# Ten weight units' rounded high part, written by a transfer from GpSimd instead of a copy on ScalarE

## The chip, the cores and the metric

The kernel runs on one core of one Trainium2 chip. The metric is the device time of one execution in microseconds (us); three runs of the kernel before gave 872.08, 871.21 and 870.69, median 871.21. A core has a matrix engine, TensorE (PE; its weight loads are listed apart as PEld), VectorE (DVE), ScalarE (ACT), GpSimd (POOL) and SyncE (SP). Each engine runs its own queue in order and waits for the others by semaphores. SP issues transfers here; after the change GpSimd does too. Results of PE land in PSUM; everything else between the steps lies in SBUF, 128 partitions wide.

## The reference

Attention in which both softmaxes come ahead of the products, followed by a dense two-layer network with the Mish function:

```python
def _attn_ref(q, k, v):            # (8, 8, 576, 64) each
    q_s = q - np.max(q, axis=-1, keepdims=True)
    q_s = np.exp(q_s)
    q_s = q_s / (np.sum(q_s, axis=-1, keepdims=True) + 1e-09)
    k_s = k - np.max(k, axis=2, keepdims=True)
    k_s = np.exp(k_s)
    k_s = k_s / (np.sum(k_s, axis=2, keepdims=True) + 1e-09)
    kv = np.einsum('bhsd,bhse->bhde', k_s, v)
    return np.einsum('bhsd,bhde->bhse', q_s, kv)

def _moe_ref(x, w_in, w_out):      # x: (4608, 512), w_in: (512, 2048), w_out: (2048, 512)
    h = x @ w_in
    sp = np.where(h > 20.0, h, np.log1p(np.exp(np.minimum(h, 20.0))))
    g = h * np.tanh(sp)
    return g @ w_out
```

x is the attention's output, heads side by side. The two weight matrices come as 64-bit floats.

## The kernel before, in words

The 4608 tokens are taken in 9 groups of 512. For each group, x is made from attention items (two heads at a time), then for 16 blocks n of 128 hidden columns: a product with w_in (`h_part`, four parts of 128 rows each), Mish on ACT (`g_mish`, "Y"), a rounded high part gh and a remainder gl (`g_hi`, `g_lo`), and a product with w_out (`out_mm`, "O"), three blocks behind. PE takes factors of the type float32r; to keep their accuracy, each factor is split in a high part (the value rounded to float32r) and a low part (value minus high part), and each product is three matmuls: high with high, high with low, low with high. So PE's third matmul of each `h_part` needs the low part of w_in (tile wil), the first two the high part (wih); in `out_mm` the first needs the high part of a w_out block (tile wo) and the second its low part.

The weights are converted on the chip. They come in 32 units of 128x512 weights: an "in" unit holds 128 columns of w_in, and its result goes into the tiles wih and wil as 128x4x128 (four pieces of 128 numbers per partition); an "out" unit holds 128 rows of w_out, and its result is a tile wo with both parts, 512 numbers in a row per partition each. The steps of unit j, each a token with its number:

- R: a load of the raw 64-bit words by SP (tiles raw_in, raw_out; line 110).
- RA: the upper word's magnitude, scaled, on ACT, into a tile wc_in or wc_out (line 117). These tiles share four buffers, so RA waits until an earlier unit's last step has freed one.
- RL or RM: the lower word, scaled, on ACT (line 121) or DVE (line 125).
- RB, then RC: the bits of both put together, then the sign, on DVE (lines 129 and 133). After RC the unit's float32 value stands in wc.
- RH: the high part, a copy on ACT into float32r (line 146, `w_hi`), shown as CAST.
- RO or RD: the low part, value minus high part, on GpSimd or DVE (line 97, `w_lo`).

From unit 17 on the units alternate: 17 in, 18 out, 19 in, 20 out and so on to 27 in; 28 to 31 are out. While the first tokens are worked on, all this is mixed with the attention items and with the first group's products. The order is not planned by rules: the string FIRST lists every step as a token, in the order of issue, and each engine's queue is the tokens that fall on it, in that order (`tc.manual_schedule`). H40 is the `h_part` of block 10, part 0 (40 = 4 x 10 + 0), and it is the first to need unit 17; H60 is block 15, part 0, the first to need unit 27. O8 and O12 are the products of out units 20 and 28; H56 is block 14, part 0. From about 130 us on the products run alone with the last attention items.

Other steps that stand beside the change: KS is the subtraction of the k maximum on DVE (line 265), E the two exponentials ke and qe on ACT (line 280), which take a table load on ACT before them, and another before the Mish that follows; Q is the q sum on DVE (lines 300 to 304) with its multiplication on GpSimd (line 309); K is the product of ke with v on PE (pkv, line 290).

Of the kernel before, what the change touches and what calls it, by code (L numbers as in the profile page):

```python
# [9 lines left out]
F32R = mybir.dt.float32r  # L10
# [30 lines left out]

STAGED = (
# [5 lines left out]
def attn_mish_mlp(ctx: ExitStack, tc: tile.TileContext, q, k, v, wu, qs, kt, out):  # L48
# [3 lines left out]
    nc = tc.nc  # L52
# [43 lines left out]
    def sub(eng, out, a, b):  # L96
        eng.tensor_tensor(out, a, b, ALU.subtract)  # L97
# [37 lines left out]
    def w_dst(j):  # L135
        kind, f = units[j]
        a = conv[j][2].bitcast(F32)
        if kind == "out" and f not in wo:
            wo[f] = xp.tile([P, 2, DM], F32R, tag=f"wo{f}", name=f"wo{f}")
        if kind == "in":  # L140
            return a.rearrange("p (t c) -> p t c", t=HP), [w[:, :, f * P:(f + 1) * P] for w in wi]
        return a, [wo[f][:, 0], wo[f][:, 1]]

    def w_hi(j):
        a, d = w_dst(j)
        nc.scalar.copy(d[0], a)  # L146

    def w_lo(j, eng):
        a, d = w_dst(j)
        sub(eng, d[1], a, d[0].bitcast(F32))  # L150
        conv.pop(j)
# [293 lines left out]
    def x_lo(i, src):  # L445
        nc.vector.tensor_tensor(xs[i][:, 1], src, xs[i][:, 0].bitcast(F32), ALU.subtract)  # L446
# [11 lines left out]
    def h_part(n, t):  # L458
        c, f = divmod(n, NF)
        if t == 0:  # L460
            gs[n] = ps_h.tile([P, 512], F32, tag="h", name=f"ph{n}")
        fs = slice(f * P, (f + 1) * P)
        x = xs[c * HP + t]
        for i, (a, z) in enumerate(((0, 0), (0, 1), (1, 0))):
            nc.tensor.matmul(gs[n], wi[a][:, t, fs], x[:, z], start=t == 0 and i == 0,  # L465
                             stop=t == HP - 1 and i == 2)
# [26 lines left out]
    def g_hi(n, copy=nc.vector.tensor_copy):  # L493
        hi = pools["rp"].tile([P, SM], F32R, tag="rh", name=f"gh{n}")
        copy(hi, gs[n])  # L495
        gs[n] = gs[n], hi
# [33 lines left out]
    def group(n):  # L530
# [58 lines left out]
        L=k_load, LK=kt_load, LQ=q_load, V=v_load, R=w_load, MK=a_kmx, MQ=a_qmax, SQ=a_qsub, SD=lambda i: a_qsub(i, nc.vector), B=a_kmax, KS=a_ksub, EK=lambda i: a_exp(i, "k"), EQ=lambda i: a_exp(i, "q"), E=a_exp, K=a_kv,  # L589
        Q=a_qsum, QM=a_qmul, QD=lambda i: a_qmul(i, nc.vector), S=a_ksum, SA=lambda i: a_kvs(i, i < HP), SB=lambda i: a_kvs(i, True), T=a_qt, TC=a_qt2, X=a_x, Z=lambda i: x_hi(i, at[i]["px"]),  # L590
        ZL=lambda i: x_lo(i, at[i]["px"]), ZT=a_tail2, ST=a_tail3, RA=w_abs, RL=w_low, RM=w_low_v, RB=w_bits, RC=w_sign,
        RH=w_hi, RO=lambda j: w_lo(j, nc.gpsimd), RD=lambda j: w_lo(j, nc.vector),
        H=lambda x: h_part(x // HP, x % HP), Y=g_mish, G=g_hi, GA=lambda n: g_hi(n, nc.scalar.copy), GL=g_lo, O=out_mm)
    with tc.manual_schedule(engines={ET.Activation, ET.PE, ET.DVE, ET.Pool, ET.SP}):
        for token in first:
# [53 lines left out]
```

## Time and profile before

| | |
|---|---|
| times of three runs | 872.08, 871.21, 870.69 us |
| profiled execution | 871.54 us, of which 869.8 us from the first to the last instruction |
| granted TensorE clock | 0.996 |
| PE, DVE, ACT, POOL busy | 848.1, 475.3, 336.4, 92.3 us |
| casts of line 146 | 32, of some 0.62 us each |
| transfers issued by GpSimd | none |

The profile is of one execution. Its page gives busy time by engine, the groups of instructions and the transfers; the timelines of one engine give for each instruction its start and length in us, its engine and line, the tile it writes and the tiles it reads, and in brackets how long the engine had idled and who released it. Equal neighbours stand in one row (x2, x3). A busy PE row of x2 holds two matmuls, of some 0.23 us each.

### The profile page before, as it was taken

The page shows a single profiled execution, that of the slowest core. Times are in us where ns is not written, and L with a number is a line of the kernel's source. Part 1 is how long each engine was busy: PE and PEld are TensorE (multiplying, and loading weights), DVE is VectorE, ACT ScalarE, POOL GpSimd, SP SyncE. Part 2 cuts the span into 40 slices and gives each one's busy share as a digit, 9 for nine tenths or more (in the row PEclk, how much of TensorE's full clock was granted, in tenths as well). Part 3 has the DMA queues.
Part 4 walks back from the last instruction along what each step waited for, and adds up shares of the span by engine and source line. Part 5 has one row for each costly group of instructions (what it writes and reads, how often), then busy time and mean ns, then how long its engine had stood idle before and what let it go on. Part 6 is the DMA issues. An engine that isn't in the chain of part 4 may idle for free.

```text
span 869.8 us, 11465 instructions
## 1 busy us (share of the span) xinstructions
PE 848.1 (98%) x4368; PEld 685.5 (79%) x4368; DVE 475.3 (55%) x1196; ACT 336.4 (39%) x509; POOL 92.3 (11%) x91
## 2 busy tenths in 40 slices
PE   5999999999999999999999999999999999999998
PEld 3677777787888878787878787878888788888886
DVE  6899997656474746465565556564743222222221
ACT  4999873424243333424342424242432111111111
POOL 4024221111111001111010111111110000000000
PEclk9899999999999999999999999999999999999999
DMA  9975344222232223212231222222200020001001
GB/s 306 388 248 194 106 132 122 71 49 60 63 103 47 72 47 105 63 54 65 91 77 31 74 76 69 51 60 61 76 18 1 15 73 13 1 0 49 1 1 49
DMA packets 73975, 69.16 MB, mean 80 GB/s; under 512 B 52928, under 2 KB 52928, under 8 KB 73920
## 3 DMA queue, kind: packets, MB, share of 16 engines
q1 hardware_dynamic: 73600, 67.91, 26.4%
q8 instruction: 34, 0.56, 0.3%
q10 hardware_dynamic: 320, 0.52, 0.2%
q14 instruction: 21, 0.17, 0.1%
HBM read 57.93 MB, written 10.49 MB: 79 GB/s over the span
## 4 chain that ended last, share of the span: by engine, by line
PE 89%; ACT 6%; SPq 1%; DVE 1%; issue 1%; DMA 1%; ACTq 0%; DVEq 0%
PE po L515 43%; PE ph L465 43%; PE pt L392 2%; PE px L380 1%; ACT L490 1%; DMA kt<-in_kt_dram 1%; ACT raw_out L121 1%; ACT wc_out L117 1%; ACT raw_in L121 1%; ACT y L490 1%; PE px L365 1%; ACT L280 0%; ACT wo L146 0%; SPq L171 0%; ACT wih L146 0%
## 5 line engine op out<-in xcount | busy, mean ns | idle before, releaser
L465 PE MATMUL ph<-xs,wih 128*128 128x512 f32 x1152 | 358.7, 393 | 3.8 <-ACT y L490 3.8
L515 PE MATMUL po<-wo,gh 128*128 128x512 f32 x1152 | 355.6, 390 | 0.3 <-POOL wo L97 0.3
L465 PEld LDWEIGHTS ph<-xs,wih 128*128 128x128 f32 x1152 | 214.0, 188 | 50.4 <-ACT y L490 5.2
L515 PEld LDWEIGHTS po<-wo,gh 128*128 128x128 f32 x1152 | 216.2, 188 | 45.5 <-POOL wo L97 0.6
L465 PE MATMUL ph<-xs,wil 128*128 128x512 f32 x576 | 225.0, 391 | 0.2 <-DVE wil L97 0.2
L515 PE MATMUL po<-wo,gl 128*128 128x512 f32 x576 | 224.4, 390 | 0.0
L490 ACT ACTIVATE y<-ph 128x512 f32<-128x512 f32 x144 | 86.1, 598 | 330.8 <-PE ph L465 261.4
L495 DVE CAST gh<-y 128x512 fp32r<-128x512 f32 x132 | 57.7, 437 | 271.0 <-ACT y L490 270.8
L465 PEld LDWEIGHTS ph<-xs,wil 128*128 128x128 f32 x576 | 108.1, 188 | 23.8 <-DVE wil L97 1.0
L515 PEld LDWEIGHTS po<-wo,gl 128*128 128x128 f32 x576 | 108.2, 188 | 22.5 <-DVE gl L97 0.2
L97 DVE TENSOR_TENSOR gl<-y,gh 128x512 fp32r<-128x512 f32 x144 | 104.6, 727 | 11.9
L490 ACT ACT_TABLE_LOAD x41 | 52.6, 1283 | 61.8 <-PE ph L465 61.6
L309 POOL TENSOR_TENSOR qe<-qe,qs 128x576 f32<-128x576 f32 (+1 forms) x31 | 36.9, 1191 | 308.8 <-DVE qs L304 290.1
L97 POOL TENSOR_TENSOR q<-q,qm 128x576 f32<-128x576 f32 (+1 forms) x30 | 35.8, 1193 | 195.8 <-DVE qm L224 183.7
L280 ACT ACT_TABLE_LOAD x29 | 37.2, 1283 | 7.0 <-DMA q<-in_q_dram 4.1
L300 DVE TENSOR_REDUCE qs<-qe 128x18 f32<-128x576 f32 (+1 forms) x32 | 24.6, 768 | 26.4 <-ACT qe L274 25.2
L520 ACT COPY ob<-po 128x512 f32<-128x512 f32 x20 | 11.7, 587 | 60.3 <-PE po L515 60.3
L446 DVE TENSOR_TENSOR xs<-px,xs 128x512 fp32r<-128x512 f32 x32 | 20.9, 685 | 17.8 <-ACT xs L443 17.8
L233 DVE TENSOR_REDUCE qm<-q 128x18 f32<-128x576 f32 (+1 forms) x32 | 24.4, 762 | 4.0 <-DMA q<-in_q_dram 3.6
L520 DVE COPY ob<-po 128x512 f32<-128x512 f32 x16 | 11.1, 691 | 26.8 <-PE po L515 26.8
L203 DVE TENSOR_REDUCE mxd<-kt 128x1 f32<-128x576 f32 x32 | 23.8, 744 | 1.0 <-DMA kt<-in_kt_dram 1.0
L280 ACT ACTIVATE ke<-k 128x640 f32<-128x640 f32 x20 | 14.8, 738 | 18.6 <-DVE k L265 18.5
(94 smaller groups left out, 516.8 us busy)
## 6 DMA issues: line engine op xcount, KB each, us to landing
k<-in_k_dram SPq DMA_DIRECT2D x32, 320.0 KB, 3.0
kt<-in_kt_dram SPq DMA_DIRECT2D x32, 288.0 KB, 2.9
raw_in<-in_w_dram SPq DMA_DIRECT2D x16, 512.0 KB, 7.6
raw_out<-in_w_dram SPq DMA_DIRECT2D x16, 512.0 KB, 4.9
out_dram<-ob SPq DMA_DIRECT2D x32, 256.0 KB, 2.2
q<-in_qs_dram SPq DMA_DIRECT2D x24, 288.0 KB, 3.0
v<-in_v_dram SPq DMA_DIRECT2D x20, 320.0 KB, 4.5
v_odd<-in_v_dram SPq DMA_DIRECT2D x12, 320.0 KB, 4.5
```

The lines of the kernel that those rows point to most:

```text
L97: eng.tensor_tensor(out, a, b, ALU.subtract)
L203: nc.vector.tensor_reduce(mxd, r["kt"], axis=AX.X, op=ALU.max)
L233: nc.vector.tensor_reduce(qm, qt, axis=AX.X, op=ALU.max)
L280: nc.scalar.activation(e.rearrange("p c h d -> p h c d"), r[nm], AF.Exp)
L300: nc.vector.tensor_reduce(z, q2, axis=AX.X, op=ALU.add)
L309: eng.tensor_tensor(q2, q2, z.unsqueeze(2).to_broadcast(list(q2.shape)), ALU.mult)
L446: nc.vector.tensor_tensor(xs[i][:, 1], src, xs[i][:, 0].bitcast(F32), ALU.subtract)
L465: nc.tensor.matmul(gs[n], wi[a][:, t, fs], x[:, z], start=t == 0 and i == 0, stop=t == HP - 1 and i == 2)
L490: nc.scalar.activation(y, gs[n], AF.Mish)
L495: copy(hi, gs[n])
L515: nc.tensor.matmul(po[t], g[a][:, t * P:(t + 1) * P], wo[f][:, z], start=f == 0 and i == 0, stop=f == NF - 1 and i == 2)
L520: copy(ob, po[t])
```

## The change

Ten units (17 and 20 to 28) have their high part written by a new step RI in place of RH: a transfer issued on GpSimd's queue, from the unit's value in SBUF to its place in wih or wo, typed float32r on both sides. The other units keep RH. The low parts of some of these units stand later in FIRST (RD17, RD20, RD25 on DVE; RO24, RO26, RO27 on GpSimd; RD23 trades places with O8). Line numbers from 147 on are 5 higher after the change.

```diff
     def w_hi(j):
         a, d = w_dst(j)
         nc.scalar.copy(d[0], a)
+
+
+    def w_hi_dma(j):
+        a, d = w_dst(j)
+        nc.gpsimd.dma_start(d[0], a.bitcast(F32R))
...
-        RH=w_hi, RO=lambda j: w_lo(j, nc.gpsimd), RD=lambda j: w_lo(j, nc.vector),
+        RH=w_hi, RI=w_hi_dma, RO=lambda j: w_lo(j, nc.gpsimd), RD=lambda j: w_lo(j, nc.vector),
...
-    "RB19 O5 E6 RC17 RB16 RB18 RC16 X5 RH17 RC18 LQ7 RH16 RD17 L7 H37 RH18 Q6 RO16 Z5 H40 ZT5 RA22 ST5 H38 ZL5 RO18 "
+    "RB19 O5 E6 RC17 RB16 RB18 RC16 X5 RI17 RC18 LQ7 RH16 L7 H37 RH18 Q6 RO16 Z5 RD17 H40 ZT5 RA22 ST5 H38 ZL5 RO18 "
...
-    "RC20 RA24 H45 GL9 RL25 H48 RH20 RC23 H46 R27 RD20 RH23 H49 RB24 RA26 H47 RB26 H50 RC24 Y11 R28 RD23 O8 GA11 "
-    "RH24 GL10 RL27 RB25 RA27 SD7 RC25 H52 R29 KS7 RO24 RH25 H51 RL28 H53 E7 RD25 O9 RC26 R30 GL11 RB27 RM29 RH26 "
-    "L8 Q7 Y12 H54 RO26 LQ8 K7 RC27 H55 V8 RA28 G12 RH27 H56 S7 QM7 KS8 Y13 O10 SB7 MQ8 RO27 RA29 RA30 RL30 GA13 T7 "
-    "RB28 H57 TC7 RB30 H60 RB29 H58 GL12 X7 RC29 RC28 RH29 H61 Z7 RC30 ZT7 H59 RH28 R31 ZL7 SQ8 RH30 ST7 H62 Y14 "
+    "RC20 RA24 H45 GL9 RL25 H48 RI20 RC23 H46 R27 RI23 H49 RB24 RD20 RA26 H47 RB26 H50 RC24 Y11 R28 O8 RD23 GA11 "
+    "RI24 GL10 RL27 RB25 RA27 SD7 RC25 H52 R29 KS7 RI25 H51 RO24 RL28 H53 E7 O9 RC26 R30 GL11 RB27 RM29 RD25 RI26 "
+    "L8 Q7 Y12 H54 LQ8 K7 RC27 H55 V8 RA28 G12 RO26 RI27 H56 S7 QM7 KS8 Y13 O10 SB7 MQ8 RA29 RA30 RL30 RO27 GA13 T7 "
+    "RB28 H57 TC7 RB30 H60 RB29 H58 GL12 X7 RC29 RC28 RH29 H61 Z7 RC30 ZT7 H59 RI28 R31 ZL7 SQ8 RH30 ST7 H62 Y14 "
```

(In the two lines of FIRST left out, RH21 and RH22 become RI21 and RI22.) PE's and SP's queues keep their order, and ACT's loses its ten casts and keeps the rest.

GpSimd's queue where the change stands, before: low parts of units 21, 22, 24 and 26, the q multiplication, the low part of unit 27.

```order
L97 TENSOR_TENSOR wil<-wc_in_999,wih 128x4x128
L97 TENSOR_TENSOR wo_1097<-wc_out_969,wo_1097 128x512
L97 TENSOR_TENSOR wo_1171<-wc_out_1116,wo_1171 128x512
L97 TENSOR_TENSOR wo_1221<-wc_out_1142,wo_1221 128x512
L309 TENSOR_TENSOR qe_1199<-qe_1199,qs_1225 128x640
L97 TENSOR_TENSOR wil<-wc_in_1177,wih 128x4x128
```

The same stretch after. The values are wc_in_999 (unit 21), wc_out_969 (22), wc_out_1034 (20), wc_in_1073 (23), wc_out_1116 (24), wc_in_1110 (25), wc_out_1142 (26) and wc_in_1177 (27).

```order
L151 DMA wih<-wc_in_999 128x4x128
L151 DMA wo_1097<-wc_out_969 128x512
L97 TENSOR_TENSOR wil<-wc_in_999,wih 128x4x128
L97 TENSOR_TENSOR wo_1097<-wc_out_969,wo_1097 128x512
L151 DMA wo_1128<-wc_out_1034 128x512
L151 DMA wih<-wc_in_1073 128x4x128
L151 DMA wo_1171<-wc_out_1116 128x512
L151 DMA wih<-wc_in_1110 128x4x128
L97 TENSOR_TENSOR wo_1171<-wc_out_1116,wo_1171 128x512
L151 DMA wo_1221<-wc_out_1142 128x512
L97 TENSOR_TENSOR wo_1221<-wc_out_1142,wo_1221 128x512
L151 DMA wih<-wc_in_1177 128x4x128
```

A transfer and a subtraction that waits for it stand in one queue: the low part of unit 22 now stands between the transfers of units 22 and 20, that of unit 24 between those of 25 and 26, and that of unit 26 ahead of the transfer of 27.

DVE's queue at unit 17, before (wc_in_842 is its value):

```order
L133 SCALAR_TENSOR_TENSOR wc_out_825<-raw_out_574,wc_out_825 128x512
L97 TENSOR_TENSOR wil<-wc_in_842,wih 128x4x128
L300 TENSOR_REDUCE qs_957<-qe_933 128x10
L303 TENSOR_SCALAR qs_957<-qs_957 128x10
L304 RECIPROCAL qs_957<-qs_957 128x10
L446 TENSOR_TENSOR xs_962<-px_939,xs_962 128x512
```

And after:

```order
L133 SCALAR_TENSOR_TENSOR wc_out_825<-raw_out_574,wc_out_825 128x512
L305 TENSOR_REDUCE qs_956<-qe_933 128x10
L308 TENSOR_SCALAR qs_956<-qs_956 128x10
L309 RECIPROCAL qs_956<-qs_956 128x10
L97 TENSOR_TENSOR wil<-wc_in_842,wih 128x4x128
L451 TENSOR_TENSOR xs_961<-px_939,xs_961 128x512
```

The subtraction for unit 17 moved behind the three steps of the q sum.

DVE's queue at unit 25 (wc_in_1110), before:

```order
L265 TENSOR_TENSOR k_950<-k_950,pb_1113 128x640
L97 TENSOR_TENSOR wil<-wc_in_1110,wih 128x4x128
L133 SCALAR_TENSOR_TENSOR wc_out_1142<-raw_out_856,wc_out_1142 128x512
L97 TENSOR_TENSOR gl_1217<-y_1152,gh_1169 128x512
L129 SCALAR_TENSOR_TENSOR wc_in_1177<-wc_in_1177,raw_in_1134 128x512
L125 TENSOR_SCALAR raw_out_1185<-raw_out_1185 128x512
L300 TENSOR_REDUCE qs_1225<-qe_1199 128x10
```

And after:

```order
L270 TENSOR_TENSOR k_949<-k_949,pb_1113 128x640
L133 SCALAR_TENSOR_TENSOR wc_out_1142<-raw_out_856,wc_out_1142 128x512
L97 TENSOR_TENSOR gl_1216<-y_1152,gh_1169 128x512
L129 SCALAR_TENSOR_TENSOR wc_in_1177<-wc_in_1177,raw_in_1134 128x512
L125 TENSOR_SCALAR raw_out_1185<-raw_out_1185 128x512
L97 TENSOR_TENSOR wil<-wc_in_1110,wih 128x4x128
L305 TENSOR_REDUCE qs_1225<-qe_1199 128x10
```

The subtraction for unit 25 moved behind four instructions and stands just ahead of the q sum, which unit 27's sign step (line 133) follows.

4 rows, old and new, of the table FIRST are left out of this document.

## The prediction

> **What bounds the kernel now.** I read the page first, then the table of stages, then the waits of TensorE, then the timelines of single engines where the change stands.
>
> ```profile
> PE 848.1 (98%) x4368; PEld 685.5 (79%) x4368; DVE 475.3 (55%) x1196; ACT 336.4 (39%) x509; POOL 92.3 (11%) x91
> 78.00:130.00 52.00, 49.86 (x250) 38.22 (x249) 49.00 (x87) 43.45 (x76) 13.93 (x10) 1.00 0.39 113
> 130.00:500.00 370.00, 368.68 (x2014) 299.37 (x2013) 220.37 (x641) 139.88 (x186) 37.12 (x32) 1.00 0.26 70
> PE ph L465 <- ACT y L490: 3.8, 3, 1.3
> PE pkv L290 <- ACT ke L280: 0.5, 1, 0.5
> L146 ACT CAST wih<-wc_in x16: 604/619/662, 24.7 to 111.8; 128x512 fp32r<-128x512 f32 x16
> L146 ACT CAST wo<-wc_out x16: 603/620/635, 37.1 to 128.3; 128x512 fp32r<-128x512 f32 x16
> ```
>
> TensorE (PE) is busy 848.1 of 869.8 us. The change can only move its 21.7 us of idling. Rows two and three are stages: limits, length, then busy time of PE, PEld, DVE, ACT, POOL, the clock, the DMA share and GB/s. All ten units are made between 78 and 130 us. There PE idles 2.1 us, but DVE works 49.00 of 52 us: the stage has two engines near their limit, and ACT (43.45) and the DMA engines (0.39) have room. Behind it PE is busy 368.68 of 370 us, so a delay that reaches PE before 130 us finds only 1.3 us to vanish in, and I count it whole. The two rows of waits say where PE waits on ACT (in 30 to 260 us); ten casts of 0.62 us leave ACT.
>
> **The change part by part.** *Removed:* ten casts, 10 x 0.62 = 6.2 us of ACT. It is worth nothing as busy time; it counts only where PE waits on ACT (step 3).
>
> *Added:* ten transfers of 256 KB inside SBUF. Each takes the place of a 0.62 us cast between a unit's sign step and its low part. The trace before has no transfer issued on GpSimd; the nearest rows are these (KB, then us from issue to landing):
>
> ```profile
> out_dram<-ob SPq DMA_DIRECT2D x32, 256.0 KB, 2.2
> kt<-in_kt_dram SPq DMA_DIRECT2D x32, 288.0 KB, 2.9
> v<-in_v_dram SPq DMA_DIRECT2D x20, 320.0 KB, 4.5
> ```
>
> The bounds are 2.2 (same size) and 4.5 us (v's rows, which the code lays in pieces of 256 bytes). An out unit moves 128 rows of 2 KB, most like kt's 128 rows of 2304 bytes: I take 2.9. An in unit writes 512 pieces of 512 bytes, between kt and v: I take 3.4. Both are estimates. So each high part comes 2.3 to 2.8 us later than by the cast; the question is which unit has that much to spare.
>
> By the Trainium skill ("DMA: Bandwidth & Descriptors", section on the anatomy of one DMA on the SWDGE path) a transfer issued on GpSimd takes 2.0 us plus its bytes over 436 GB/s, an estimate of 2.6 us here for either kind. No row here can show it yet. By the sensitivity given below the sum would be about +1.1 us and not +2.5.
>
> *Step 1, unit 17 (the part of H40).*
>
> ```profile
> 81.74 0.50 PE L465 MATMUL ph<-xs,wil 128*128 128x512 f32 x1
> 77.84 0.68 DVE L133 SCALAR_TENSOR_TENSOR wc_in<-raw_in,wc_in 128x512 uint32<-128x512 uint32 x1
> 80.99 0.69 DVE L97 TENSOR_TENSOR wil<-wc_in,wih 128x512 fp32r<-128x512 f32 x1
> 81.60 0.81 DVE L300 TENSOR_REDUCE qs<-qe 128x10 f32<-128x640 f32 x1
> 82.92 0.22 DVE L304 RECIPROCAL qs<-qs 128x10 f32<-128x10 f32 x1
> 83.05 0.63 DVE L446 TENSOR_TENSOR xs<-px,xs 128x512 fp32r<-128x512 f32 x1
> ```
>
> The subtraction of the low part (80.99) goes behind the q sum, which takes 81.60 to 83.05. PE's product with wil, at 81.74, comes 83.05 - 81.60 = 1.45 later. The transfer can start at 77.84 + 0.68 = 78.52 and lands at 81.9, before that subtraction; PE's products with wih wait for it too, inside the 1.45.
>
> *Step 2, units 22 and 20 (the O8 product).* On GpSimd the order is now: transfer 22, low part 22, transfer 20. GpSimd runs its queue in order, so transfer 20 waits until transfer 22 has landed and its subtraction is done: two landings in series.
>
> ```profile
> 92.73 0.68 DVE L133 SCALAR_TENSOR_TENSOR wc_out<-raw_out,wc_out 128x512 uint32<-128x512 uint32 x1
> 94.15 1.31 POOL L97 TENSOR_TENSOR wo<-wc_out,wo 128x512 fp32r<-128x512 f32 x1 [2.49 <-ACT wo L146]
> 98.00 0.69 DVE L97 TENSOR_TENSOR wo<-wc_out,wo 128x512 fp32r<-128x512 f32 x1 [0.79 <-ACT wo L146]
> 99.49 0.62 PE L515 MATMUL po<-wo,gh 128*128 128x512 f32 x2
> ```
>
> Unit 22's sign ends at 93.41; + 2.9 = 96.3; + 1.31 = 97.6; + 2.9 = 100.5; + 0.69 on DVE = 101.2. PE's second O8 product, at some 99.7, waits until then: +1.5. This isn't added to step 1: both push the same clock of PE, and the later one wins.
>
> *Step 3, does ACT's gift arrive?* Unit 26's first step (line 117) reuses a buffer that unit 20's subtraction frees.
>
> ```profile
> 98.72 0.69 ACT L117 ACTIVATE wc_out<-raw_out 128x512 f32<-128x512 f32 x1 [0.24 <-DVE wo L97]
> 99.45 0.69 DVE L129 SCALAR_TENSOR_TENSOR wc_out<-wc_out,raw_out 128x512 uint32<-128x512 uint32 x1 [0.15 <-ACT wc_out L117]
> 101.47 1.63 POOL L97 TENSOR_TENSOR wo<-wc_out,wo 128x512 fp32r<-128x512 f32 x1 [6.02 <-ACT wo L146]
> 101.86 1.79 DVE L129 SCALAR_TENSOR_TENSOR wc_in<-wc_in,raw_in 128x512 uint32<-128x512 uint32 x1
> 105.05 0.33 SPq L110 DMA_DIRECT2D raw_out<-in_w_dram  x1
> 108.33 0.44 DVE L125 TENSOR_SCALAR raw_out<-raw_out 128x512 uint32<-128x512 uint32 x1 [0.15 <-DMA raw_out<-in_w_dram]
> 104.91 0.81 DVE L265 TENSOR_TENSOR k<-k,pb 128x640 f32<-128x640 f32 x1
> 107.53 0.74 ACT L280 ACTIVATE ke<-k 128x640 f32<-128x640 f32 x1
> 108.32 0.81 PE L290 MATMUL pkv<-v,ke 128*64 128x66 f32 x20 [0.51 <-ACT ke L280]
> 105.55 0.67 ACT L121 ACTIVATE raw_out<-raw_out 128x512 uint32<-128x512 uint32 x1
> 106.24 1.28 ACT L280 ACT_TABLE_LOAD   x1
> 108.80 0.61 ACT L146 CAST wo<-wc_out 128x512 fp32r<-128x512 f32 x1
> 111.37 0.73 PE L465 MATMUL ph<-xs,wih 128*128 128x512 f32 x2 [1.34 <-ACT y L490]
> ```
>
> That row moves from 98.72 to 101.2, and DVE's in-order queue behind it (99.45) starts at about 102.0, 2.5 late. One thing is won back: at 101.86 a DVE operation that takes 0.69 elsewhere took 1.79 beside GpSimd's of 101.47; that subtraction now runs later, so 1.1 goes there. The k subtraction (104.91) is 1.4 late and ends at 107.2. Unit 24's sign step, on DVE right behind 99.45, now ends at 103.3 and frees a raw buffer; a load takes 3.3 (issued 105.05, in at 108.33), so unit 28's raw words are in at 106.6. ACT's step on them and a table load (0.67 and 1.28) stand ahead of ke, which starts at 108.6 instead of 107.53: 1.1 late. Then qe, then no cast (the one of 108.80 is gone, 0.62 back), then y: 0.5 late, and so PE's product of 111.37. So the two waits of 0.51 and 1.34 us, the only ones here that ACT's time could shorten, do not vanish: +0.5 at this place.
>
> *Step 4, units 25 and 27 (the part of H60).*
>
> ```profile
> 110.96 0.63 DVE L133 SCALAR_TENSOR_TENSOR wc_in<-raw_in,wc_in 128x512 uint32<-128x512 uint32 x1
> 111.50 1.48 DVE L495 CAST gh<-y 128x512 fp32r<-128x512 f32 x1
> 112.67 1.47 POOL L97 TENSOR_TENSOR wil<-wc_in,wih 128x512 fp32r<-128x512 f32 x1
> 116.59 0.39 PE L465 MATMUL ph<-xs,wil 128*128 128x512 f32 x1
> ```
>
> Before, wil of unit 27 is ready at 112.67 + 1.47 = 114.14, 2.45 early. Now unit 27's sign (110.96 to 111.59) is followed by 3.4 of landing and 1.47 of GpSimd: 116.5, no spare. And it is late itself: unit 25's sign ends 1.4 late at 106.4, its transfer lands at 109.8, and its subtraction now stands ahead of the q sum and of unit 27's sign on DVE, which then ends at 113.1 (+1.5). Landing 116.55, low part 118.0: +1.45. In GpSimd's queue the low part of 24 now falls on unit 26's sign step; if it blocks DVE as at 101.86, 1.1 more: +2.5. I take +2.5, as the row of 101.86 shows that blocking whenever the two meet.
>
> *Step 5, unit 28 (O12).*
>
> ```profile
> 119.73 1.88 DVE L133 SCALAR_TENSOR_TENSOR wc_out<-raw_out,wc_out 128x512 uint32<-128x512 uint32 x3
> 122.25 1.89 DVE L97 TENSOR_TENSOR wo<-wc_out,wo 128x512 fp32r<-128x512 f32 x3
> 124.08 0.61 PE L515 MATMUL po<-wo,gh 128*128 128x512 f32 x2
> ```
>
> Its sign, second of three, ends at 121.0; landing 123.9, subtraction 124.6, against 124.14 before: 0.4 late, covered by the 2.5 PE already lost. Uncovered it would cost 0.3, as 0.17 is spare. Units 21, 23 and 24 end in waits that lie inside steps 2 to 4.
>
> *Sum.* 1.45, 1.5, 0.5 and 2.5 are successive positions of one clock, so the last stays: 871.54 + 2.5 = **874.0** (the profiled run; the median of all three is 871.21, 0.33 lower). Steps 2 to 4 hold two out landings and one in landing in series, so each microsecond on all landings moves the sum by 3.
>
> **The rivals.**
> *Nothing changes.* With landings of 2.2 (the out_dram row) unit 20 is ready at 93.41 + 2.2 + 1.31 + 2.2 + 0.69 = 99.8, on time; the 1.1 of blocking at 101.86 pays for the 1.1 by which unit 26 is late, and unit 27's low part is ready by about 115.5, inside its spare time. Step 1's 1.45 remains in PE's clock but eats the 0.51 and 1.34 of waiting: 871.5. For it: that row has the very size. Against: it is issued from another queue.
>
> *Faster.* Landings of 2.2 or less, GpSimd's blocking stays away at 101.86, and the casts' time reaches PE: both waits, 0.51 and 1.34, go: 871.54 - 1.85 = 869.7. More isn't on offer, as PE idles 2.1 in the whole stage. Against it: step 1's 1.45 hangs on order alone and would have to be made good as well, and at O12 (step 5) DVE has only 0.17 spare and the 1.1 of blocking to come earlier by.
>
> *Slower, by held-up issuing.* DVE and GpSimd block each other: DVE's cast of 111.50 took 1.48 beside GpSimd's work. If GpSimd's issuing is held likewise under a long DVE operation, landings go to v's 4.5: 2 x 1.6 + 1.1 = 4.3 more, 878.3. For it: DVE works 94% of this stage. Against: GpSimd's subtraction at 94.15 took its usual 1.31, though DVE was busy beside it.
>
> The Trainium skill ("SBUF — State Buffer", section on the two separate sides) has this as a rule that speaks against the change: while DVE runs a copy or cast in its two-port mode, GpSimd cannot write descriptors, and its transfers stand. The trace agrees as far as that 1.48, and no run shows it for a transfer yet.
>
> *Not what it says.* A transfer that copied unrounded would leave a low part of zero, with the same time as the forecast.
>
> **How the numbers follow.** Forecast (landings near 2.9 and 3.4) 0.48, its own range 872.3 to 876; nothing changes 0.31; held-up issuing 0.13; faster 0.08. The measurement can tell about 0.2%, or 1.74 us. The held-up case and most of the forecast lie above that; the forecast's low end, 872.3 to 873.3, does not, and I count 0.05 of it to no change: slower 0.56, no change 0.36, faster 0.08. The range 870.4 to 878.8 takes in both bounds of the landing and leaves out the faster case and a late end beyond 4.5.
>
> **What would show it.** The GpSimd transfers' issue-to-landing row: 2.9 and 3.4, or 2.2, or 4.5. PE waiting on wil for some 1.4 at 81.7 (step 1), on wo of unit 20 for 1 to 1.5 at O8 (step 2), on y at H56 (step 3), and on wil of unit 27 at H60 (step 4); PE's idle time in 78 to 130 up from 2.1 to 4.6 and the later stages unchanged. Landings under 2.4 or a wait-free O8 would make the forecast wrong; so would idling after 130 us.

## The result and the profile after

The changed kernel takes 877.46 us (median of 4 runs, 876.02 to 879.33) against 870.95 us before (4 runs): a ratio of 1.0082, 95% interval 1.0070 to 1.0095. It is slower by 6.5 us. The profiled execution took 877.89 us, 876.1 of them from first to last instruction.

Three views of the changed kernel: busy time on the page; the table of stages (limits, length, busy time of PE, PEld, DVE, ACT and POOL, clock, DMA share, GB/s); and the rows of PE's waits from 30 to 260 us that the change touched (waited for: us in total, times, longest).

```profile
PE 848.2 (97%) x4368; PEld 684.2 (78%) x4368; DVE 476.3 (54%) x1196; ACT 331.9 (38%) x499; POOL 99.6 (11%) x101
78.00:130.00 52.00, 44.77 (x217) 33.00 (x215) 42.85 (x76) 34.04 (x61) 20.34 (x20) 0.97 0.55 146
130.00:500.00 370.00, 368.45 (x2012) 299.01 (x2011) 222.61 (x643) 140.65 (x186) 37.17 (x32) 1.00 0.26 71
PE ph L470 <- ACT y L495: 2.4, 2, 1.3
PE pq L349 <- POOL qe L314: 1.7, 1, 1.7
PE ph L470 <- DVE wil L97: 1.7, 1, 1.7
PE ph L470 <- DMA wih<-wc_in: 1.6, 2, 1.1
PE pkv L295 <- ACT ke L285: 1.1, 1, 1.1
PE po L520 <- DMA wo<-wc_out: 0.9, 1, 0.9
```

PE works as long as before (848.2 us), and from 130 to 500 us as densely. The loss lies where the ten units are made: PE's 49.86 busy us there are 44.77 now. ACT's busy time fell, and nothing came of it. New releasers of PE are the transfers themselves, GpSimd's q multiplication and the low part of unit 17. The clock's mean is 0.97 in that stage.

Up to the first changed step both programs are the same, yet the product px just ahead of it (line 365 before, 370 after) starts at 79.26 us in the one profile and at 77.72 in the other: executions differ in their first stage. So places are counted from that product, in us, read from PE's timelines:

| place on PE | before | after | later by |
|---|---|---|---|
| low product of unit 17 (H40) | 2.48 | 4.91 | 2.4 |
| pkv of item 6 | 4.98 | 8.76 | 3.8 |
| pkv of item 7 | 29.06 | 32.81 | 3.8 |
| unit 25, first product (H56) | 32.11 | 35.59 | 3.5 |
| q transpose of item 7 (pq, line 344 / 349) | 35.63 | 41.16 | 5.5 |
| low product of unit 27 (H60) | 37.33 | 43.22 | 5.9 |
| unit 28, second product (O12) | 45.05 | 52.62 | 7.6 |
| end of the span | 790.54 | 798.38 | 7.8 |

The loss comes in three pieces: 3.8 at unit 17, 2.1 at the q transpose of item 7 and just behind it, 1.7 at unit 28. (Some 0.3 more behind O12 is not placed. The start was 1.5 earlier in this profile, so the spans differ by 6.3 and not by 7.8.)

**Piece one, unit 17.** PE, DVE and GpSimd in the timelines of the changed kernel:

```profile
80.20 0.73 PE L470 MATMUL ph<-xs,wih 128*128 128x512 f32 x2 [0.55 <-DMA wih<-wc_in]
82.63 0.50 PE L470 MATMUL ph<-xs,wil 128*128 128x512 f32 x1 [1.70 <-DVE wil L97]
83.79 1.05 PE L470 MATMUL ph<-xs,wih 128*128 128x512 f32 x2
80.98 1.59 DVE L97 TENSOR_TENSOR wil<-wc_in,wih 128x512 fp32r<-128x512 f32 x1
79.52 2.50 POOL L97 TENSOR_TENSOR wo<-wc_out,wo 128x512 fp32r<-128x512 f32 x2 [1.32 <-ACT wo L146]
81.99 1.70 POOL L314 TENSOR_TENSOR qe<-qe,qs 128x640 f32<-128x640 f32 x1
83.00:87.00 4.00, 4.00 (x20) 2.78 (x20) 3.41 (x13) 2.42 (x4) 0.70 (x1) 0.57 0.00 0
```

PE waits 0.55 us for the transfer and 1.70 for the subtraction. This one starts right behind the q sum, 1.5 us later after px than before, and took 1.59 us instead of 0.69 beside GpSimd's work: together the 2.4. Then two matmuls take 1.05 us in place of 0.62: in the last row, the stretch from 83 to 87 us, the granted clock is 0.57. So 2.4 us of delay are 3.8 by the time pkv of item 6 starts.

**Pieces two and three.** The first two rows are from the view of transfers (KB, median us from issue to landing). Then come SP's raw loads, GpSimd's queue and who waited for it.

```profile
wih<-wc_in POOLq DMA_DIRECT2D x5, 256.0 KB, 2.9
wo<-wc_out POOLq DMA_DIRECT2D x5, 256.0 KB, 4.0
103.20 4.83 SPq L110 DMA_DIRECT2D raw_out<-in_w_dram  x3
106.81 0.76 POOL L151 DMA_DIRECT2D wih<-wc_in  x1 [2.61 <-DVE wc_in L133]
109.93 0.76 POOL L151 DMA_DIRECT2D wo<-wc_out  x1
113.20 0.69 DVE L97 TENSOR_TENSOR wil<-wc_in,wih 128x512 fp32r<-128x512 f32 x1 [2.63 <-DMA wih<-wc_in]
115.25 1.53 POOL L97 TENSOR_TENSOR wo<-wc_out,wo 128x512 fp32r<-128x512 f32 x1 [4.55 <-DMA wo<-wc_out]
116.73 0.80 POOL L151 DMA_DIRECT2D wih<-wc_in  x1
114.86 0.22 DVE L309 RECIPROCAL qs<-qs 128x10 f32<-128x10 f32 x1
117.55 1.27 POOL L314 TENSOR_TENSOR qe<-qe,qs 128x640 f32<-128x640 f32 x1
118.88 0.65 PE L349 MATMUL pq<-ident,qe 128*128 128x128 f32 x4 [1.71 <-POOL qe L314]
125.61 0.59 POOL L151 DMA_DIRECT2D wo<-wc_out  x1 [4.73 <-DVE wc_out L133]
129.62 0.49 PE L520 MATMUL po<-wo,gh 128*128 128x512 f32 x1 [0.91 <-DMA wo<-wc_out]
104.00:116.00 12.00, 9.77 (x58) 7.30 (x57) 8.00 (x15) 6.72 (x9) 3.98 (x5) 1.00 0.97 276
```

The same q multiplication, the same q transpose and the same stretch in the kernel before:

```profile
111.21 1.50 POOL L309 TENSOR_TENSOR qe<-qe,qs 128x640 f32<-128x640 f32 x1 [0.45 <-DVE qs L304]
114.89 0.60 PE L344 MATMUL pq<-ident,qe 128*128 128x128 f32 x4
104.00:116.00 12.00, 10.14 (x63) 7.88 (x62) 11.52 (x20) 10.49 (x17) 4.20 (x3) 1.00 0.56 167
```

Unit 25's transfer, issued at 106.81, is in at 113.2 (6.4 us); unit 26's, at 109.93, at 115.2 (5.3); unit 28's, at 125.61, at 129.6 (4.0). In the stretch from 104 to 116 us the DMA engines are 97% busy (56% before), with three raw loads of 512 KB among others. The q multiplication (117.55) needs none of the transfers ahead of it, and its q sum was done at 115.1 (114.86 and 0.22), but it stands behind them in GpSimd's queue: the low part of 26 waited 4.55 us for its landing, then the transfer of 27 was issued, then came the multiplication, and PE waited 1.71 for that.

### The profile page after: what moved, and what is told of

It is laid out like the page before. It is cut to its first block, busy times and chain, and to the rows that moved or that the text cites. A ratio compares the mean times of both kernels' runs of the same rounds, so it can differ in the third digit from the quotient of the medians.

```text
span 876.1 us, 11488 instructions
## 1 busy us (share of the span) xinstructions
PE 848.2 (97%) x4368; PEld 684.2 (78%) x4368; DVE 476.3 (54%) x1196; ACT 331.9 (38%) x499; POOL 99.6 (11%) x101
## 4 chain that ended last, share of the span: by engine, by line
PE 87%; ACT 4%; DVE 2%; DMA 2%; issue 2%; SPq 1%; POOL 1%; POOLq 0%; DVEq 0%; ACTq 0%
PE po L520 42%; PE ph L470 41%; PE pt L397 2%; DMA kt<-in_kt_dram 1%; PE px L385 1%; ACT L495 1%; ACT wc_out L117 0%; DMA wo<-wc_out 0%; ACT y L495 0%; DVE wc_in L133 0%; ACT raw_in L121 0%; ACT raw_out L121 0%; DMA raw_in<-in_w_dram 0%; PE pt L385 0%; SPq L176 0%
```

## The experiments

Two theories stood at the start. By *order*, the moved subtractions cost the time. By *late landing*, it is the transfers: either since they share the DMA engines with SP's loads, or since VectorE holds GpSimd's issuing up. The diffs of 1, 7 and 10 stand against the changed kernel, the others against the kernel before. A kernel is compared with the kernel before on the same chip: 870.73 us in the first group, 871.22 in the second, 869.91 in the third (medians of 15, 23 and 19 runs).

**1. The order alone.** RI becomes RH again; FIRST stays as changed.

```diff
-... X5 RI17 RC18 LQ7 RH16 L7 H37 RH18 Q6 RO16 Z5 RD17 H40 ...
+... X5 RH17 RC18 LQ7 RH16 L7 H37 RH18 Q6 RO16 Z5 RD17 H40 ...
```

> The changed order, but all ten high parts are copied by ScalarE as before: no transfer on GpSimd. If the transfers' landing times carry the 6.5 us, only the moved subtraction of unit 17 is left (its product waits some 1.5 us at 82), and the two waits on ScalarE at 108 and 111 (0.51 and 1.34 us) take most of that up: -0.5 to +1.5 us against the kernel before. If the moved subtractions themselves are the cause: +5 to +6.5 us.

Measured: 873.72 us, 1.0032 (1.0019 to 1.0044), runs from 871.53 to 874.13. Both figures missed: the order costs some 3 us by itself, nearly half of the loss. In its profile the low product of unit 17 comes 5.36 us after px, 2.9 later than before and even later than with the transfer: beside GpSimd's low parts the second step of the q sum took 1.16 us (0.68 in the changed kernel), and the subtraction 1.59 in both.

```profile
83.14 0.50 PE L470 MATMUL ph<-xs,wil 128*128 128x512 f32 x1 [2.91 <-DVE wil L97]
```

The profile is of the fastest execution, in which PE's clock didn't fall: from px to the end of the span it is 791.92 us, only 1.4 more than before. That the runs spread over 2.6 us led to experiment 11.

**2. Units 17 and 20 to 23 alone**, with their moved subtractions (the first four changed lines of FIRST; the last three as before).

```diff
-... X5 RH17 RC18 LQ7 RH16 RD17 L7 H37 ... RH21 ... RH22 ... RH20 ... RH23 ...
+... X5 RI17 RC18 LQ7 RH16 L7 H37 ... RI21 ... RI22 ... RI20 ... RI23 ...
```

> Only units 17 and 20 to 23 by transfers, with their moved subtractions; 24 to 28 by ScalarE in the order of before. Theory that loads on the same DMA engines make the transfers late: nearly no load is under way then, landings 2.5 to 3.0 us, and the time +0.5 to +2.5 us. Theory that a transfer's issuing is held up by VectorE, which is as busy here as later: landings of 4 us and more and +3 us or more. If each half carries half of the loss: +3 us.

Measured: 875.76 us, 1.0062 (1.0049 to 1.0074): +5.0. Its transfers land in 2.3 to 3.9 us, at a median of 2.8, so but for one (unit 23's, 3.9) the landings are as the theory of the loads has them, and the price is not: short landings too cost 5 us here. PE stands 4.5 us late at pkv of item 6 and 5.0 at pkv of item 7, where two rows of its timeline show that the two waits on ACT of the kernel before are all there; the row ahead of them is the clock behind unit 17:

```profile
83.00:87.00 4.00, 4.00 (x10) 2.80 (x9) 3.45 (x13) 2.03 (x3) 0.72 (x1) 0.50 0.00 0
111.75 0.81 PE L295 MATMUL pkv<-v,ke 128*64 128x66 f32 x20 [1.19 <-ACT ke L285]
114.79 0.73 PE L470 MATMUL ph<-xs,wih 128*128 128x512 f32 x2 [1.34 <-ACT y L495]
```

PE's delay was not taken up by them, since ACT, which they wait for, was as late. So in this profile nearly all of the 5 us stands at unit 17 already: 2.45 us at its low product, and 2.1 more up to pkv of item 6 with the clock at 0.50. What units 20 to 23 add shows against experiment 4, where a delay of 4.0 us at that place is taken up by half.

**3. Units 24 to 28 alone** (the last three changed lines).

```diff
-"RH24 GL10 ... KS7 RO24 RH25 H51 RL28 H53 E7 RD25 O9 ... RM29 RH26 "
+"RI24 GL10 ... KS7 RI25 H51 RO24 RL28 H53 E7 O9 ... RM29 RD25 RI26 "
```

> Only units 24 to 28 by transfers, with their moved subtractions; 17 and 20 to 23 as before. Theory of the loads on the same DMA engines: landings of 24, 25, 26 and 28 at 4 to 6 us, as in the whole change, and +3.5 to +5.5 us. Theory that the chain through units 22 and 20 starts the loss: +1 us or less, since that chain is as before here.

Measured: 873.08 us, 1.0028 (1.0017 to 1.0038): +2.4, between the two. Landings of 2.7 to 4.5 us. Here the waits on ACT at item 7 do shrink, as the change lets ACT start ke earlier: PE is 1.5 us *ahead* at H56 (first row). It loses that and 2.3 more behind it, 2.8 of the 3.8 in three waits (the other rows):

```profile
108.81 0.73 PE L470 MATMUL ph<-xs,wih 128*128 128x512 f32 x2 [0.39 <-ACT y L495]
114.65 0.66 PE L349 MATMUL pq<-ident,qe 128*128 128x128 f32 x4 [2.14 <-POOL qe L314]
117.03 0.50 PE L470 MATMUL ph<-xs,wil 128*128 128x512 f32 x1 [0.46 <-POOL wil L97]
125.37 0.50 PE L520 MATMUL po<-wo,gh 128*128 128x512 f32 x1 [0.22 <-DVE wo L97]
```

**4. Unit 17 alone.**

```diff
-... X5 RH17 RC18 LQ7 RH16 RD17 L7 H37 RH18 Q6 RO16 Z5 H40 ...
+... X5 RI17 RC18 LQ7 RH16 L7 H37 RH18 Q6 RO16 Z5 RD17 H40 ...
```

> Only unit 17 by a transfer, its subtraction behind the q sum. It lands in some 2.9 us, the product with its low part waits 1.5 to 1.7 us at 82 and PE's clock drops for about 3 us behind it, as in the changed kernel. If the waits at 108 and 111 take a delay up: -0.3 to +0.7 us in all. If a delay of PE at 82 goes to the end whole: +1.5 to +3 us.

Measured: 872.72 us, 1.0025 (1.0015 to 1.0035): +2.0. The transfer lands in 2.9 us and PE waits 0.52 and 1.70, as in the whole change; the clock falls as well. PE is 4.0 late at pkv of item 6 and 2.2 late at H56: about half is taken up, and half goes to the end.

**5 and 6. Without three raw loads**, on the kernel before and on the change.

```diff
+        if j in (28, 29, 30):
+            conv[j] = list(raw[j - 4])
+            return
         st = xp.tile([P, SM, 2], U32, tag=STAGED.split()[j], name=f"raw_{kind}{f}")
```

> The kernel before without the raw loads of units 28, 29 and 30 (three times 512 KB on SP, the ones of 101 to 108 us); these units use the raw words of units 24, 25 and 26 a second time, so their weights are not the reference's. It is the base for the next run. Without the wait for the load the exponentials of ke stand no earlier than the k subtraction: -0.3 to -1.5 us against the kernel before.

> The changed kernel with the same three loads left out, the weights of units 28 to 30 likewise not the reference's. Theory of the loads on the same DMA engines: the landings of 24, 25 and 26 fall from 4.7, 6.4 and 5.3 us to 2.5 to 3.2, and the time is within 1.5 us of the run without loads before it. Theory that VectorE or GpSimd's own work holds the issuing up: the landings stay at 4.5 us and more, and the difference stays 5 to 6.5 us.

Measured: 870.93 us without the change, 0.9997 (0.9989 to 1.0006), and 875.41 with it, 1.0056 (1.0039 to 1.0074). So the change costs 4.5 us without these loads and 6.5 with them. The profiled execution of the changed one took 879.36 us, the five others 874.22 to 875.75, and PE's clock stood at 0.50 from 84 to 90 us in it; so landings and waits are read from it, and not the total. Its view of transfers and its timeline:

```profile
wo<-wc_out POOLq DMA_DIRECT2D x5, 256.0 KB, 2.7
113.02 0.57 POOL L156 DMA_DIRECT2D wo<-wc_out  x1 [0.87 <-DVE wc_out L138]
116.39 1.35 POOL L97 TENSOR_TENSOR wo<-wc_out,wo 128x512 fp32r<-128x512 f32 x1 [2.80 <-DMA wo<-wc_out]
118.51 1.27 POOL L319 TENSOR_TENSOR qe<-qe,qs 128x640 f32<-128x640 f32 x1
119.83 0.66 PE L354 MATMUL pq<-ident,qe 128*128 128x128 f32 x4 [1.69 <-POOL qe L319]
```

The out units' median falls from 4.0 to 2.7, and unit 26 lands in 3.4 us in place of 5.3 (113.02 to 116.39); unit 25 lands in 2.9 in place of 6.4, and PE's wait on that transfer is gone. That speaks for the theory of shared DMA engines, and not for that of held-up issuing: from 104 to 116 us VectorE was busier without the loads (10.88 of 12 us, 8.00 with them) and the landings were shorter, and in the changed kernel VectorE even stood idle for 2.63 us ahead of 113.20 while unit 25's transfer was under way. But the total missed that theory's figure of 1.5 us: late landings beside these loads account for some 2 us of 6.5, and as the intervals of the two ratios just touch, that size is rough. PE's wait for the q multiplication stays (1.69), since the low part of 26 and the transfer of 27 still stand ahead of it on GpSimd.

**7. All ten transfers in the old order.**

```diff
-... X5 RI17 RC18 LQ7 RH16 L7 H37 RH18 Q6 RO16 Z5 RD17 H40 ...
+... X5 RI17 RC18 LQ7 RH16 RD17 L7 H37 RH18 Q6 RO16 Z5 H40 ...
```

(and likewise in the other lines: every RH of the kernel before that the change replaces becomes RI, and nothing moves.)

> All ten transfers, but the order of the kernel before: every subtraction stands where it stood. VectorE then waits at the subtractions of 17 and 25 until they land, with its bit and sign steps queued behind, and GpSimd's transfer of 25 stands behind the low part of 24. If the moved subtractions are a help: +8 to +11 us. If they are what costs: +2 us or less.

Measured: 880.72 us, 1.0113 (1.0098 to 1.0129): +9.5, the figure for moves that help. They cost at unit 17 (its low product comes 3.64 us after px here, 4.91 in the changed kernel) and save more later. DVE stands still until unit 25 lands, and PE waits long for the q multiplication behind it:

```profile
111.02 0.69 DVE L97 TENSOR_TENSOR wil<-wc_in,wih 128x512 fp32r<-128x512 f32 x1 [4.67 <-DMA wih<-wc_in]
121.04 1.12 PE L349 MATMUL pq<-ident,qe 128*128 128x128 f32 x4 [5.81 <-POOL qe L314]
```

**8. No transfers, but three ACT steps moved** behind the exponentials: what did ACT have to give?

```diff
-"... KS7 RO24 RH25 H51 RL28 H53 E7 RD25 O9 RC26 R30 GL11 RB27 RM29 RH26 "
-"L8 Q7 Y12 H54 RO26 LQ8 ...
+"... KS7 RO24 H51 H53 E7 RH25 O9 RC26 R30 GL11 RB27 RM29 RD25 "
+"L8 Q7 Y12 RL28 RH26 H54 RO26 LQ8 ...
```

> No transfer on GpSimd. The kernel before, with ScalarE's copies of units 25 and 26 and its scaling for unit 28 moved behind the exponentials of item 7 (copy 25) and behind the Mish that follows (the other two), and the low part of 25 behind them on VectorE. If ScalarE's order there causes PE's waits of 0.51 and 1.34 us at 108 and 111, both shrink: -0.5 to -1.8 us. If VectorE takes the lead at once (0.17 us to spare at the product of unit 28): -0.2 us or nothing.

Measured: 870.21 us, 0.9996 (0.9986 to 1.0006): no difference that can be told. PE's two waits on ACT are gone and two others stand in their place, 0.45 for the q multiplication on GpSimd and 0.50 for unit 28's low part on DVE.

**9. Unit 17 by a transfer, its subtraction in the old place.**

```diff
-... X5 RH17 RC18 LQ7 RH16 RD17 L7 H37 ...
+... X5 RI17 RC18 LQ7 RH16 RD17 L7 H37 ...
```

> Only unit 17 by a transfer, and its subtraction where it stood before, ahead of the q sum. If the moved subtraction is what costs at unit 17: the product with its low part waits 0.4 us instead of 1.7, PE's clock stays at 1.00 behind it, and the waits at 108 and 111 take the delay up: -0.5 to +0.7 us. If the transfer itself is what costs: +2 us, as with the subtraction moved.

Measured: 871.61 us, 1.0024 (1.0011 to 1.0037): +1.7, about what the transfer costs with the subtraction moved. In the profiled execution (871.25 us) PE waits 0.62 and 0.46 at unit 17, its clock stays at 1.00, and yet the delay of 1.3 us goes to the end whole (rows below). Three of the eight executions took 874.0 to 874.2 us, two of them at a mean clock of 0.993, so the clock isn't out of play in the median.

```profile
80.06 1.16 DVE L97 TENSOR_TENSOR wil<-wc_in,wih 128x512 fp32r<-128x512 f32 x1 [0.80 <-DMA wih<-wc_in]
107.81 0.81 PE L295 MATMUL pkv<-v,ke 128*64 128x66 f32 x20 [0.46 <-ACT ke L285]
110.86 0.73 PE L470 MATMUL ph<-xs,wih 128*128 128x512 f32 x2 [1.35 <-ACT y L495]
```

DVE waited 0.80 for the transfer and lost 0.47 beside GpSimd; its queue leads to ke and y, so the waits on ACT moved along at their old length (0.46 and 1.35) instead of taking the delay up.

**10. The change without unit 17.**

```diff
-... X5 RI17 RC18 LQ7 RH16 L7 H37 RH18 Q6 RO16 Z5 RD17 H40 ...
+... X5 RH17 RC18 LQ7 RH16 RD17 L7 H37 RH18 Q6 RO16 Z5 H40 ...
```

> The whole change but for unit 17, which is copied by ScalarE with its subtraction in the old place: nine transfers. If the delays are positions of one clock of PE, of which the last counts: the chain through units 22 and 20 now stops PE itself at its product (1.5 to 2.5 us at 100), and the end stays late by +4.5 to +6 us. If they add up: the 2.2 us of unit 17 alone go away, +4.3 us, with no wait at unit 20's product.

Measured: 875.47 us, 1.0058 (1.0045 to 1.0071): +5.6. So taking unit 17 out, which costs 2.0 alone, saves 0.9: the delays are successive positions of PE's time more than a sum. But the wait is not where it was expected: at unit 20's product PE waits 0.30 and not 1.5 to 2.5. The large wait is for unit 25's transfer:

```profile
99.21 0.50 PE L520 MATMUL po<-wo,gh 128*128 128x512 f32 x1 [0.30 <-DVE wo L97]
111.91 1.19 PE L470 MATMUL ph<-xs,wih 128*128 128x512 f32 x2 [2.42 <-DMA wih<-wc_in]
```

**11. The kernel of experiment 1 once more**, with one more profile.

> The changed order with all copies on ScalarE once more, as its times spread from 871.5 to 874.1 us and its profile was of the fastest. If PE's granted clock falls in some executions only, behind one and the same wait at unit 17: a time of 873.5 us or more goes with matmuls of 0.6 us and a clock near 0.5 from 83 to 87 us, and a time near 871.5 with a clock of 1.00. If the clock has no part in the spread: 873.5 us with a clock of 1.00.

Measured: 872.32 us, between the two times given, so the thresholds missed; but the clock is there. The stretch from 83 to 87 us in experiment 1 and in this one, the same kernel behind the same wait of 2.9 us (columns as above, the clock third from the end):

```profile
83.00:87.00 4.00, 3.86 (x33) 3.02 (x34) 3.65 (x14) 3.67 (x6) 1.21 (x1) 1.00 0.00 0
```

```profile
83.00:87.00 4.00, 4.00 (x16) 2.89 (x17) 3.51 (x13) 2.22 (x4) 0.80 (x1) 0.57 0.00 0
```

33 matmuls at a clock of 1.00, 16 at 0.57. From px to the end of the span it is 791.92 us in the one and 793.07 in the other: 1.2 more. The two ran on different chips, but the five executions of experiment 1, all on one chip, go the same way: 871.53 and 872.30 us at mean clocks of 0.998 and 0.997, and 873.72 to 874.13 us at 0.995 and 0.996. So part of the order's 3 us is the clock's.

**12. No transfers, and more steps moved.** As experiment 8, and the two waits that it left are taken on: GpSimd's low part of 26 goes behind that of 27 and so behind the q multiplication, and unit 28 is finished ahead of 29 and 30 (with unit 30's first steps on ACT a little later).

```diff
-... RO27 RA29 RA30 RL30 GA13 T7 "
-"RB28 H57 TC7 RB30 H60 RB29 H58 GL12 X7 RC29 RC28 RH29 H61 Z7 RC30 ZT7 H59 RH28 ...
-"RD29 O11 E8 RD30 RD28 ...
+... RO27 RO26 RA29 GA13 T7 "
+"RB28 H57 TC7 RA30 RL30 RB29 H60 RB30 H58 GL12 X7 RC28 RC29 RH28 H61 Z7 RC30 ZT7 H59 RH29 ...
+"RD28 O11 E8 RD29 RD30 ...
```

> No transfer on GpSimd. As the run with the late copies, and moreover GpSimd's low part of 26 behind that of 27 (its q multiplication comes first, where PE waited 0.45 us), and unit 28's sign, copy and low part ahead of those of 29 (where PE waited 0.50 us). If these two were what took the gain back: -1.0 to -2.0 us against the kernel before, and no wait over 0.3 us from 100 to 125 us. If VectorE is the limit of the stage: another wait appears and the gain stays under 0.7 us.

Measured: 868.40 us, 0.9983 (0.9975 to 0.9992): 1.5 us faster than the kernel before. No wait of PE over 0.17 us is left from 78 to 130 us, and PE is busy 51.45 of the 52 us there:

```profile
78.00:130.00 52.00, 51.45 (x256) 39.53 (x255) 48.35 (x91) 41.90 (x75) 14.47 (x10) 1.00 0.38 115
```

## Why the prediction was right and where it was not

The direction was right and so, in outline, was the reason: transfers that come later than the casts delay PE in one stage, and nothing behind that stage makes it good. The size was not: +6.5 us in place of the forecast's 2.5, outside its own range of 872.3 to 876, with PE idle for 7.2 us from 78 to 130 us where 4.6 were forecast. That the wide range (870.4 to 878.8) held 877.46 is partly luck: it reached that far for the rival of held-up issuing (878.3), and that rival's price came by another mechanism.

- *Step 1* was mis-sized. The 1.45 us of the moved subtraction measured 2.4, as the subtraction took 1.59 us and not 0.69 beside GpSimd; the transfer's own wait of 0.55 lies inside that, as forecast. The clock's fall, worth 1.3 more, was not in the sum. The order alone costs 3 us (experiment 1), part of which is the clock's.
- *Step 2* was right in its chain and wrong in its price. Units 22 and 20 landed in series, in 3.0 and 2.6 us. But the sum took the time of unit 22's sign from the profile before. In experiment 10 that sign comes 1.1 us earlier after px: two bit steps of VectorE ahead of it took 1.28 us together, and 2.38 before, when GpSimd's low part of unit 21 ran beside them. The two landings were 2.3 and 2.5 us there. So PE's wait is 0.30 where unit 17 doesn't cover it, and none in the changed kernel: the wait-free O8 that the prediction had named as a sign against it.
- *Step 3* was right that the waits on ACT don't vanish (1.15 us for ke in the changed kernel), and far too low in its delay: PE is 3.5 us late at H56 and not 0.5. ACT's step on unit 28's raw words starts 3.7 us late after px, as the load that it waits for was issued 3.9 us late and took 4.5 us in place of 3.3; ke and y come 3.8 and 3.2 late behind it. PE's wait at H56 is put down to unit 25's transfer, but y was done only 0.2 us ahead of that landing, so the transfer added little there. What ACT's freed time can give shows in experiment 3, where PE came 1.5 us ahead.
- *Step 4* named the right units and the wrong place. The low part of 26 ahead of the transfer of 27 was in the order; what I left out is that the q multiplication stands behind both in the same queue. PE's wait is at that q transpose (1.71 us), and only 0.4 is added at H60. The 1.1 us for GpSimd's low part of 24 beside unit 26's sign didn't come: the sign took 0.68 us (at 106.96), and the low part started behind it, at 108.43. Nor do the two engines block one another whenever they meet: before, GpSimd's step of 94.15 took its usual 1.31 us, and VectorE's beside it, of 93.94 and 94.70, took 0.81 and 0.69, as elsewhere.
- *Step 5* failed by its landing: 4.0 us and not 2.9. A raw load is issued 0.4 us behind it; that this load is the reason wasn't tested for this unit. What was to be 0.4 us under cover is 1.7 in the open.
- *Landings.* Some 2.9 holds for units 17, 20, 21, 22 and 27 (2.5 to 3.0), for in units as well, where I had 3.4. It fails beside raw loads: 4.0 to 6.4 for units 23 to 26 and 28 (unit 20's, with a raw load issued 0.6 us behind it, still took 2.5). The estimate took medians of SP's transfers, and what was missing was the DMA share at the time: 0.39 on average in the stage before, but already 0.82 from 108 to 112 us there, and 0.97 from 104 to 116 us after. By the Trainium skill's rule ("DMA: Bandwidth & Descriptors", section on the anatomy of one DMA) my estimate was 2.6; the quiet landings of 2.5 to 3.0 agree with it, and the total doesn't follow from it.
- *The rival of held-up issuing.* The rule of the Trainium skill that I set beside it ("SBUF — State Buffer", section on the two separate sides) was not seen at work on a transfer: the longest landing had VectorE idle for its last 2.6 us. What was seen is that steps of the two engines can stretch one another: VectorE's subtraction took 1.59 us and not 0.69 beside GpSimd's.
- *"Nothing changes"* supposed landings of 2.2. With landings of 2.3 to 2.9, and one of 3.9, experiment 2 still costs 5 us; landings of 2.2 throughout were not run. *"Faster"* supposed that ACT's time reaches PE: in experiment 8 both waits on ACT went, and nothing was gained.

Open stays how much of the loss belongs to each of units 20 to 23, which weren't run one by one. How much of the medians' differences comes from the clock is open too, since it falls in some executions only. No run moved the q multiplication ahead of the low part of 26 in the changed kernel: that its place in the queue costs PE 1.71 us is read from the timeline.

## What to carry to other kernels

A cast handed to a transfer puts 2.3 to 6.5 us in the place of 0.6, and everything behind the waiting consumer in an in-order queue pays: look at what stands behind it there, related or not, before looking at the engine that is relieved. An estimate of a landing is worth little where the DMA engines are busier than where it was read: units 24 to 26 took 2.7 to 3.3 us without the three loads beside them and 4.7 to 6.4 with them. Moving two of these casts and one scaling step a little later on their own engine, and then the steps that PE waited for next, won 1.5 us where ten transfers lost 6.5.

## What the runs showed of the hardware

- A transfer issued by GpSimd keeps GpSimd busy for 0.53 to 0.76 us with 128 pieces of 2 KB and 0.75 to 0.94 with 512 pieces of 512 bytes, and both land in about the same time when the DMA engines are free: 2.6 and 2.9 us in experiment 2.
- PE's clock fell to 0.50 for 3 us and more behind waits of 2.2 to 2.9 us at unit 17, for the 2.9 us in one execution of a kernel and not in another (experiments 1 and 11). Over the 4 us behind them it was also 0.57 after a wait of 2.42 us (experiment 10, from 111 us) and after two of 0.52 and 1.33 us with 1.7 us of matmuls between (experiment 5, from 109 us). It stayed at 1.00 behind 0.51 and 1.34 us at the same place in the kernel before, behind 2.14 us (experiment 3) and behind 0.62 and 0.46 us (experiment 9). The Trainium skill ("TensorE: Matmul & The Clock Gate", part 1) says that the clock halves after an idle window of about 3.4 us and that the window runs freely. That one and the same wait met it or not agrees with a free-running window; that 2.2 us of waiting in two pieces with work between were enough (unit 17 in the changed kernel) is shorter than the page's figure, and there the measurement decides.
- Steps of GpSimd and VectorE that run side by side can stretch one another: 0.69 to 1.59 us for a subtraction on VectorE (unit 17), 1.30 to 1.83 for one on GpSimd (unit 22's low part).
